# An attention kernel with a feed-forward: five token chunks get the first product of both halves in Strassen's form

## The chip, the cores and the metric

The kernel runs on one core of a Trainium2 chip. The metric is the device time of one execution in microseconds (us); below, every number without a unit is in us. TensorE multiplies matrices, VectorE and ScalarE work element by element and read TensorE's results from PSUM, GpSimd (POOL in the profile) does element work in SBUF alone, and SyncE (SP) issues most transfers. Each engine takes its instructions in the order in which the program gives them.

## The reference

`q`, `k` and `v` are 8 x 8 x 576 x 64 (batch, head, position, dimension), `w_in` is 512 x 2048 and `w_out` 2048 x 512, all float32.

```python
q_s = exp(q - max(q, -1)); q_s /= sum(q_s, -1)
k_s = exp(k - max(k, 2));  k_s /= sum(k_s, 2)
kv  = einsum('bhsd,bhse->bhde', k_s, v)
a   = einsum('bhsd,bhde->bhse', q_s, kv)
x   = a.transpose(0, 2, 1, 3).reshape(4608, 512)
h   = x @ w_in
out = (h * sigmoid(h)) @ w_out
```

Attention is linear: each batch needs a small 64 x 64 matrix `kv` per head. Most of the work is the two products behind it, `x @ w_in` (the first product) and the product with `w_out` (the second).

## The kernel before

**Tiles.** The 4608 tokens are nine chunks of 512 (`TCH`; chunk 0 is worked as the 576 tokens of batch 0). For each chunk, `x` stands transposed in `XT` (features on partitions), the activated first product in `GT` (2048 features as 16 blocks of 128, by tokens), in two buffers that alternate. PSUM has eight banks: 0 to 3 take the first product, 4 and 5 the second, 6 and 7 the attention.

**The first product** has two forms. Plain (`mm1`, L288): per block of 128 features four matmuls 128 x 512 into one bank, then tanh on ScalarE (L248) and a multiply on VectorE (L249), or for the first three blocks one silu on ScalarE (L293). Strassen's (`group`, L352): a half of the features (8 blocks, `g` = 1 or 0) as seven products M1 to M7, in the order 1, 2, 6, 5, 7, 4, 3. Each is eight matmuls 128 x 256. M1, M6, M7 and M4 pile up in banks 0 and 1; M2 takes banks 2 and 3 alone, and M5, M3 pile up there. After M1, M6 and M7 the sum so far is copied out ("snapshot", `group_snap`, L341) to `h0`, `h1`, `h2`; after M2, M7 and M3 VectorE adds banks 2 and 3 to `h0`, `h2`, `h1` (`group_add`, L344). A silu on ScalarE (L350) of each of these, and one directly of banks 0 and 1 after M4, gives the four quarters of the output. The operands are differences of quarters of `x` (`XS1` to `XS4`, `xs_op`, L328, once per chunk) and of `w_in` (`WS`, `ws_op`, L319, once per half).

**The second product** of the chunk before (`prod`, L463) is in Strassen's form throughout: seven products of two parts, each part eight matmuls 128 x 256, in the same order, with differences of `GT` (`S1` to `S4`, `s_op`, L437; S3 is made in place) and of `w_out` (`T1` to `T4`, `t_op`, L447; T3 is made in place too). Its snapshots `sa`, `sb`, `sc` are ScalarE's (L479), its output adds VectorE's (L483, L494), and its stores go through SP.

**The attention** of the next batch runs beside: loads of q, k, v (L97); exps on ScalarE (L108, L111); row sums and reciprocals on VectorE (L146, L150); the scaling of q on POOL (`qnorm`, L155); a cast of v on POOL (`vcast`, L91); a transposing transfer on SP (L165); the `kv` matmuls (L187) with a scaling on VectorE (L198, L200); and `xt` (L226), the matmuls that give `XT` for the next chunk, copied out by VectorE for the first half of the features and by ScalarE for the second.

**The order.** All of it is written out by hand. `units` is a list of pieces of TensorE work: a `p` is one plain block, a `g` one of M1 to M7, a `b` one part of a product of the second kind. `plan(u, f)` puts the work `f` ahead of unit `u`. A chunk 2 to 6 has the pattern

```python
four_pairs = "ggbgbgbgbbgbgb"
"pbpbpbpbpbpbpbp" + four_pairs     # chunks 2 to 6: 29 units
four_pairs + four_pairs            # chunks 7 and 8: 28 units
```

so in chunks 2 to 6 one half of the features is plain, the other (`g` = 1) in Strassen's form. Chunk 1 mixes plain blocks (units 10 to 31 from its start, two banks while the second product of chunk 0 holds four) with that product.

Of the kernel before, what the change touches and what calls it, by code (L numbers as in the profile page):

```python
# [17 lines left out]
def kernel(  # L18
# [252 lines left out]
    hb = [0, 2]  # L271
# [16 lines left out]
    def mm1(t, fb, one=False):  # L288
        bank = hb[0] % hb[1]
        hb[0] += 1  # L290
        mm1_mm(t, fb, bank, range(NC))
        if one:
            nc.scalar.activation(  # L293
                out=GTS[t % 2][:, fb, 0:TCH], in_=PS[:, bank, :], func=ACT.Silu, scale=1.0 / XS
            )
        else:
            mm1_silu(t, fb, bank)
# [41 lines left out]
    def group_snap(i):  # L339
        H[i] = mp.tile([128, 2 * TCH], FP32, name=f"h{i}", bufs=1)  # L340
        nc.scalar.copy(out=H[i], in_=PS[:, 0:2, :].rearrange("p b n -> p (b n)"))  # L341
# [10 lines left out]
    def group(t, g, i):  # L352
# [11 lines left out]
        for p in range(4):  # L364
            for c in range(2):
                nc.tensor.matmul(  # L366
                    out=PS[:, bank + p // 2, (p % 2) * HT:(p % 2 + 1) * HT],
                    lhsT=a[:, c, p * 128:(p + 1) * 128],
                    rhs=bb[:, c, :],
                    start=(i in (1, 2, 5) and c == 0 and p % 2 == 0),  # L370
                    stop=(i in (2, 3, 4) and c == 1 and p % 2 == 1),
                    skip_group_check=True,
                )
        if i == 1:
            group_snap(0)
        elif i == 2:
            group_add(0)
        elif i == 6:
            group_snap(1)
        elif i == 7:  # L380
            group_snap(2)
            group_add(2)
        elif i == 4:
            group_silu(t, None, f1, 0)
        elif i == 3:
            group_silu(t, 2, f1, 1)
            group_silu(t, 0, f0, 0)
            group_add(1)
# [232 lines left out]
    def a_units(t):  # L621
        return [lambda t=t, fb=fb: mm1(t, fb) for fb in FB]

# [13 lines left out]
    a1 = a_units(1)  # L637
# [4 lines left out]
    units += a1[NFB - 10:]  # L642
    for t in range(2, NCH):
        begin[t] = len(units)
        bs = b_units(t - 1, ORDER)
        free = t + 1 >= B
        ps_ = [
            lambda t=t, i=i, fb=fb: mm1(t, fb, i < 3)
            for i, fb in enumerate(() if free else (0, 8, 1, 9, 2, 10, 3, 11))
        ]  # L650
        gs = [
            lambda t=t, g=g, i=i: group(t, g, i)
            for g in ((1, 0) if free else (1,))
            for i in (1, 2, 6, 5, 7, 4, 3)
        ]
        plan(begin[t] + 2, lambda t=t: s_op(t - 1, 1))
        plan(begin[t] + 4, lambda t=t: s_op(t - 1, 2))
        plan(begin[t] + (5 if free else 15), lambda t=t: s_op(t - 1, 3))
        plan(begin[t] + 21, lambda t=t: s_op(t - 1, 4))
        four_pairs = "ggbgbgbgbbgbgb"  # L660
        for x in (four_pairs if free else "pbpbpbpbpbpbpbp") + four_pairs:
            units.append({"p": ps_, "b": bs, "g": gs}[x].pop(0))
            if x == "g" and len(gs) % 7 == 0:
                later = 1 if t == NCH - 1 and not gs else 3
                f0 = 8 if free and not gs else 12
                plan(len(units) - 1 + later, lambda t=t, f0=f0: group_silu(t, 1, f0, 1))
        assert not (ps_ or bs or gs)
        x = begin[t] + (0 if free else 1)
        plan(x, lambda t=t: (xs_op(t, 1), xs_op(t, 2), xs_op(t, 3), xs_op(t, 4)))
# [98 lines left out]
    plan(b1 + 22, lambda: (mm2_plain_out(0, (0, 1)), hb.__setitem__(0, 2), hb.__setitem__(1, 3)))  # L768
# [4 lines left out]
    plan(begin[2], lambda: (hb.__setitem__(0, 0), hb.__setitem__(1, 4)))  # L773
    plan(begin[2] + 5, lambda: t_op(3, nc.vector))
    plan(begin[2] + 18, lambda: t_op(4, nc.vector, 0, 4))
    plan(begin[2] + 20, lambda: t_op(4, nc.vector, 4, 8))

    for t in range(2, NCH - 1):
        b = t + 1
        u = begin[t]  # L780
        if b < B:
            for i in range(2):
                plan(u + 5 + i, lambda i=i, b=b: exp_q(b, i))
                plan(u + 6 + 3 * i, lambda i=i, b=b: (qsum(b, i), qnorm(b, i, nc.gpsimd)))
                plan(u + 10 + 2 * i, lambda i=i, b=b: vcast(b, i, nc.gpsimd))
                plan(u + 17 + 2 * i, lambda i=i, b=b: exp_k(b, i))
                if b + 1 < B:
                    plan(u + 7 + i, lambda i=i, b=b: load(b + 1, "qt", q, i, nc.sync))
                    plan(u + 18 + i, lambda i=i, b=b: load(b + 1, "vt", v, i, nc.sync))
                    plan(u + 20 + i, lambda i=i, b=b: load(b + 1, "kt", k, i, nc.sync))  # L790
            plan(u + 13, lambda b=b: q_transpose(b))
            plan(u + 22, lambda b=b: kv_both(b))
        if b == B:
            plan(u + 8, lambda: (ws_op(1, 0), ws_op(2, 0)))
            plan(u + 11, lambda: (ws_op(3, 0), ws_op(4, 0)))
        plan(u + (24 if b < B else 23), lambda t=t: xt(t + 1, 0, nc.vector))
        plan(u + (27 if b < B else 26), lambda t=t: xt(t + 1, 1))
# [36 lines left out]
```

The softmax here doesn't subtract the row's maximum and nothing guards it: scores larger than these inputs give would overflow.

## Time and profile before

| what | value |
|---|---|
| time, median of 12 runs (lowest, highest) | 270.18 (269.64, 271.05) |
| the profiled execution: its time, its span | 270.61, 268.8 |
| TensorE matmuls, busy | 259.3 (96%) |
| VectorE, ScalarE, POOL, busy | 199.8 (74%), 184.8 (69%), 71.6 (27%) |
| granted TensorE clock | 1.000 |
| bytes moved | 45.88 MB |

A profile line of a group gives the line of the code, the engine, the operation, output<-input with shapes and count; then busy time and mean ns of one; then the idle time just ahead of these on the engine and what ended it. A line of the timeline gives start and duration in us, engine, line, operation and count, and in brackets idle time with its releaser. The line of a window gives the stretch, its length, and for each engine busy time and number of instructions; then granted clock, share of DMA and GB/s. Matmuls overlap, so differences of starts tell what one costs. `PE` is TensorE, `PEld` its weight loads, `DVE` VectorE, `ACT` ScalarE.

### The profile page before, as it was taken

How to read it: one execution, taken by the hardware profiler on the slowest of the kernel's cores; microseconds unless marked ns; L12 is line 12 of the kernel's file. 1: busy time of each engine (PE TensorE's matmuls, PEld its weight loads, DVE VectorE, ACT ScalarE, POOL GpSimd, SP SyncE). 2: the span in 40 equal slices, each digit the busy share in tenths (PEclk: the TensorE clock that was granted, in tenths of full speed). 3: DMA queues.
4: the chain of work that ended last, by engine and by line, in shares of the span. 5: the costliest groups of instructions: out<-in, count | busy, mean ns of one | idle time of the engine just before them, and what ended most of it. 6: DMA issues, size and time to landing. Idle time of an engine off the chain costs nothing.

```text
span 268.8 us, 6167 instructions
## 1 busy us (share of the span) xinstructions
PE 259.3 (96%) x2588; PEld 189.3 (70%) x2588; DVE 199.8 (74%) x279; ACT 184.8 (69%) x226; POOL 71.6 (27%) x63
## 2 busy tenths in 40 slices
PE   8899999999999999999999999999999999999993
PEld 2467644445678767876687668766878888888782
DVE  2866796978898769776977698759869838855832
ACT  5767955669866896689668966896686756674610
POOL 1743981730082007300740064005500000000004
PEclk9999999999999999999999999999999999999999
DMA  7999999399549844993598458940415003400534
GB/s 257 322 206 354 255 336 332 151 212 391 201 148 262 255 93 166 190 329 83 178 231 284 86 176 197 306 97 0 90 35 124 2 0 66 93 0 5 122 76 117
DMA packets 35452, 45.88 MB, mean 171 GB/s; under 512 B 16208, under 2 KB 19984, under 8 KB 35424
## 3 DMA queue, kind: packets, MB, share of 16 engines
q1 hardware_dynamic: 29568, 33.69, 45.1%
q0 software_dynamic: 5616, 11.60, 16.5%
q8 instruction: 20, 0.33, 0.5%
q10 hardware_dynamic: 240, 0.20, 0.3%
q14 instruction: 8, 0.07, 0.1%
HBM read 36.70 MB, written 9.44 MB: 172 GB/s over the span
## 4 chain that ended last, share of the span: by engine, by line
PE 66%; DVE 12%; DMA 6%; ACT 6%; issue 6%; POOL 2%; POOLq 0%; DVEq 0%; ACTq 0%
PE PS L463 28%; PE PS L366 18%; PE PS L276 11%; DMA qt<-in_q_dram 5%; DVE zq L146 4%; DVE GT L249 4%; PE PS L401 3%; ACT eq L108 2%; PE PS L226 2%; PE PS L187 2%; ACT L108 2%; DMA W<-in_moe_w_in_dram 1%; ACT sg L248 1%; DVE ow L483 1%; DVE h L344 1%
## 5 line engine op out<-in xcount | busy, mean ns | idle before, releaser
L463 PEld LDWEIGHTS <-GT 128*128 128x128 f16 x512 | 49.6, 98 | 11.7 <-issue 1.8
L155 POOL TENSOR_TENSOR eq<-eq,rzq 128x1152 bf16<-128x1152 bf16 x13 | 27.5, 2116 | 105.1 <-DVE rzq L150 105.1
L276 PE MATMUL PS<-XT,W 128*128 128x512 f16 (+1 forms) x224 | 54.7, 371 | 0.3 <-ACT ow L413 0.3
L463 PE MATMUL PS<-W,GT 128*128 128x256 f16 x384 | 49.1, 273 | 0.4 <-DVE h L344 0.4
L344 DVE TENSOR_TENSOR h<-PS,h 128x1024 f32<-128x1024 f32 x27 | 33.0, 1221 | 17.9 <-PE PS L366 10.4
L249 DVE SCALAR_TENSOR_TENSOR GT<-sg,PS 128x512 f16<-128x512 f32 (+2 forms) x57 | 37.4, 671 | 10.8 <-ACT sg L248 10.2
L248 ACT ACTIVATE sg<-PS 128x512 f32<-128x512 f32 (+2 forms) x57 | 33.1, 595 | 17.2 <-PE PS L276 8.1
L463 PEld LDWEIGHTS <-S 128*128 128x128 f16 x384 | 37.5, 98 | 7.7
L341 ACT COPY h<-PS 128x1024 f32<-128x1024 f32 x27 | 27.3, 1013 | 18.6 <-PE PS L366 18.4
L276 PEld LDWEIGHTS <-W 128*128 128x128 f16 x224 | 21.7, 98 | 17.2 <-issue 1.3
L463 PE MATMUL PS<-T,S 128*128 128x256 f16 x256 | 32.7, 273 | 0.0
L366 PEld LDWEIGHTS <-WS 128*128 128x128 f16 x288 | 27.3, 98 | 4.7 <-issue 1.4
L366 PE MATMUL PS<-XS,WS 128*128 128x256 f16 x216 | 28.0, 273 | 0.0
L350 ACT ACTIVATE GT<-h 128x1024 f16<-128x1024 f32 x27 | 27.5, 1055 | 0.3 <-DVE h L344 0.3
L146 DVE TENSOR_REDUCE zq<-eq 128x18 f32<-128x1152 bf16 x12 | 16.2, 1350 | 15.2 <-ACT eq L108 15.2
L366 PEld LDWEIGHTS <-W 128*128 128x128 f16 x216 | 21.1, 98 | 5.4 <-issue 2.0
L696 POOL DMA_DIRECT2D out_dram<-ow x5 | 2.7, 546 | 70.8 <-DVE ow L681 70.8
L108 ACT ACTIVATE eq<-qt 128x1152 bf16<-128x1152 f32 x16 | 18.1, 1158 | 2.7 <-DMA qt<-in_q_dram 2.6
L91 POOL CAST vaug<-vt 128x1152 bf16<-128x1152 f32 x12 | 19.4, 1647 | 0.0
L111 ACT ACTIVATE ek<-kt 128x1152 bf16<-128x1152 f32 x16 | 18.6, 1164 | 1.2 <-DMA kt<-in_k_dram 1.2
L366 PE MATMUL PS<-XT,W 128*128 128x256 f16 x144 | 18.2, 272 | 0.9 <-DVE h L344 0.4
L256 PE MATMUL PS<-XT,W 128*128 128x288 f16 x128 | 16.6, 286 | 1.0 <-DVE GT L249 0.6
(78 smaller groups left out, 341.1 us busy)
## 6 DMA issues: line engine op xcount, KB each, us to landing
out_dram<-ow SPq DMA_DIRECT2D x64, 128.0 KB, 2.4
qt<-in_q_dram SPq DMA_DIRECT2D x12, 576.0 KB, 4.6
kt<-in_k_dram SPq DMA_DIRECT2D x12, 576.0 KB, 7.8
vt<-in_v_dram SPq DMA_DIRECT2D x12, 576.0 KB, 5.8
qt<-in_q_dram POOLq DMA_DIRECT2D x4, 576.0 KB, 13.5
kt<-in_k_dram POOLq DMA_DIRECT2D x4, 576.0 KB, 13.8
vt<-in_v_dram POOLq DMA_DIRECT2D x4, 576.0 KB, 12.3
W<-in_moe_w_out_dram POOLq DMA_DIRECT2D x4, 512.0 KB, 15.1
```

Source lines behind the costliest of these rows:

```text
L91: eng.tensor_copy(o, i)
L108: nc.scalar.activation(out=half(st[b]["eq"], cc), in_=jgd(b, "qt", cc), func=ACT.Exp)
L146: nc.vector.reduce_sum(out=z, in_=e, axis=AX.X)
L155: eng.tensor_tensor(out=e, in0=e, in1=r[:, :, :, None].to_broadcast([128, J, 2, D]), op=ALU.mult)
L248: nc.scalar.activation(out=s, in_=i, func=ACT.Tanh, scale=OS)
L249: nc.vector.scalar_tensor_tensor(out=o, in0=s, scalar=1.0, in1=i, op0=ALU.add, op1=ALU.mult)
L276: nc.tensor.matmul(out=PS[:, bank, o0:TCH], lhsT=W1[:, c, fb * 128:(fb + 1) * 128], rhs=XTS[t % 2][:, c, o0:TCH], start=(c == 0), stop=(c ...
L341: nc.scalar.copy(out=H[i], in_=PS[:, 0:2, :].rearrange("p b n -> p (b n)"))
L344: nc.vector.tensor_tensor(out=H[i], in0=PS[:, 2:4, :].rearrange("p b n -> p (b n)"), in1=H[i], op=ALU.add)
L350: nc.scalar.activation(out=group_out(t, f, n), in_=x, func=ACT.Silu, scale=1.0 / XS)
L366: nc.tensor.matmul(out=PS[:, bank + p // 2, (p % 2) * HT:(p % 2 + 1) * HT], lhsT=a[:, c, p * 128:(p + 1) * 128], rhs=bb[:, c, :], start=(i ...
L463: nc.tensor.matmul(out=PS[:, bank, m * HN:(m + 1) * HN], lhsT=a[:, fc, m * 128:(m + 1) * 128], rhs=bb[:, fc, :], start=(first and fc == 0) ...
```

## The change

Chunks 2 to 6 get the pattern of chunks 7 and 8: both halves in Strassen's form, 28 units. A new function `full(t)` lays out such a chunk:

- Of the six snapshots two are VectorE's: the second of half 1 (after M6) and the third of half 0 (after M7).
- The silus of `h0`, `h1`, `h2` are no longer issued right after M3 but at units of their own (`defer`); that of half 0's `h1` falls at the start of the next chunk.
- All four exps stand ahead of unit 11 (units 3, 4, 6 and 10), where they stood at units 5, 6, 17 and 19. The loads of q and k for the batch after that follow the exps; those of v come at units 22 and 23.
- Row sums at units 7 and 11; scaling on POOL behind them; casts of v at units 2 and 11; the transpose at 17; `kv` at 15 (22 before); `xt` at 22 and 27 (24 and 27 before).
- `s_op` at units 4, 5, 15 and 19 (2, 4, 15 and 21 before).

Outside: the weight differences of half 0 (`ws_op(.., 0)`) move from chunk 7 to units 10 and 11 of chunk 1; T4 and T3 move from VectorE in chunk 2 to POOL at unit 22 of chunk 1; chunk 1's plain blocks take their banks from a list. On POOL the casts of a batch now come ahead of its scalings.

The diff, cut to its core:

```diff
-    hb = [0, 2]
+    A1_BANKS = [0, 1, 0, 1, 0, 1, 2, 0, 3, 1, 0, 2, 1, 0, 2, 3]
 
...
-    def mm1(t, fb, one=False):
-        bank = hb[0] % hb[1]
-        hb[0] += 1
-        mm1_mm(t, fb, bank, range(NC))
-        if one:
-            nc.scalar.activation(
-                out=GTS[t % 2][:, fb, 0:TCH], in_=PS[:, bank, :], func=ACT.Silu, scale=1.0 / XS
-            )
-        else:
-            mm1_silu(t, fb, bank)
+    def mm1(t, i):
+        mm1_mm(t, FB[i], A1_BANKS[i], range(NC))
+        mm1_silu(t, FB[i], A1_BANKS[i])
 
 
 
...
-    def group_snap(i):
+    def group_snap(i, eng=nc.scalar):
         H[i] = mp.tile([128, 2 * TCH], FP32, name=f"h{i}", bufs=1)
-        nc.scalar.copy(out=H[i], in_=PS[:, 0:2, :].rearrange("p b n -> p (b n)"))
+        copy(eng, H[i], PS[:, 0:2, :].rearrange("p b n -> p (b n)"))
 
...
-    def group(t, g, i):
+    def group(t, g, i, on=None, defer=False):
...
+        on = on or {}
         if i == 1:
             group_snap(0)
         elif i == 2:
             group_add(0)
         elif i == 6:
-            group_snap(1)
+            group_snap(1, on.get(1, nc.scalar))
         elif i == 7:
-            group_snap(2)
+            group_snap(2, on.get(2, nc.scalar))
             group_add(2)
         elif i == 4:
             group_silu(t, None, f1, 0)
         elif i == 3:
-            group_silu(t, 2, f1, 1)
-            group_silu(t, 0, f0, 0)
+            if not defer:
+                group_silu(t, 2, f1, 1)
+                group_silu(t, 0, f0, 0)
             group_add(1)
 
 
...
     ORDER = (1, 2, 6, 5, 7, 4, 3)
-    a1 = a_units(1)
+    a1 = [lambda i=i: mm1(1, i) for i in range(NFB)]
 
     units += [lambda i=i: mm2_plain(0, i) for i in range(10)]
     for i in range(10, NFB):
         units += [a1[i - 10], lambda i=i: mm2_plain(0, i)]
     units += a1[NFB - 10:]
+    four_pairs = "ggbgbgbgbbgbgb"
+    def full(t):
+        begin[t] = u = len(units)
+        b = t + 1
+        bs = b_units(t - 1, ORDER)
+        gs = [
+            lambda g=g, i=i: group(t, g, i, {1: nc.vector} if g else {2: nc.vector}, True)
+            for g in (1, 0)
+            for i in ORDER
+        ]
+        for x in 2 * four_pairs:
+            units.append({"b": bs, "g": gs}[x].pop(0))
+        for i, x in ((1, 4), (2, 5), (3, 15), (4, 19)):
+            plan(u + x, lambda i=i: s_op(t - 1, i))
+        for g, at3 in ((1, (13, 17, 15)), (0, (23, 28, 25))):
+            f1, f0 = 4 * g, 4 * g + 8
+            for i, x, f, n in zip(range(3), at3, (f0, f0, f1), (0, 1, 1)):
+                plan(u + x, lambda i=i, f=f, n=n: group_silu(t, i, f, n))
+        more = b + 1 < B
+        for i in range(2):
+            plan(u + (3, 10)[i], lambda i=i: exp_q(b, i))
+            plan(u + (7, 11)[i], lambda i=i: qsum(b, i))
+            plan(u + (16, 17)[i], lambda i=i: qnorm(b, i, nc.gpsimd))
+            plan(u + (2, 11)[i], lambda i=i: vcast(b, i, nc.gpsimd))
+            plan(u + (6, 4)[i], lambda i=i: exp_k(b, i))
+            if more:
+                plan(u + (5, 12)[i], lambda i=i: load(b + 1, "qt", q, i, nc.sync))
+                plan(u + (8, 6)[i], lambda i=i: load(b + 1, "kt", k, i, nc.sync))
+                plan(u + (22, 23)[i], lambda i=i: load(b + 1, "vt", v, i, nc.sync))
+        plan(u + 17, lambda: q_transpose(b))
+        plan(u + 15, lambda: kv_both(b))
+        plan(u + 22, lambda: xt(t + 1, 0, nc.vector))
+        plan(u + 27, lambda: xt(t + 1, 1))
+        plan(u, lambda: (xs_op(t, 1), xs_op(t, 2), xs_op(t, 3), xs_op(t, 4)))
     for t in range(2, NCH):
-        begin[t] = len(units)
+        if t < B - 1:
+            full(t)
+            continue
+        begin[t] = u = len(units)
         bs = b_units(t - 1, ORDER)
-        free = t + 1 >= B
-        ps_ = [
-            lambda t=t, i=i, fb=fb: mm1(t, fb, i < 3)
-            for i, fb in enumerate(() if free else (0, 8, 1, 9, 2, 10, 3, 11))
-        ]
-        gs = [
-            lambda t=t, g=g, i=i: group(t, g, i)
-            for g in ((1, 0) if free else (1,))
-            for i in (1, 2, 6, 5, 7, 4, 3)
-        ]
-        plan(begin[t] + 2, lambda t=t: s_op(t - 1, 1))
-        plan(begin[t] + 4, lambda t=t: s_op(t - 1, 2))
-        plan(begin[t] + (5 if free else 15), lambda t=t: s_op(t - 1, 3))
-        plan(begin[t] + 21, lambda t=t: s_op(t - 1, 4))
-        four_pairs = "ggbgbgbgbbgbgb"
-        for x in (four_pairs if free else "pbpbpbpbpbpbpbp") + four_pairs:
-            units.append({"p": ps_, "b": bs, "g": gs}[x].pop(0))
+        gs = [lambda t=t, g=g, i=i: group(t, g, i) for g in (1, 0) for i in ORDER]
+        plan(u + 2, lambda t=t: s_op(t - 1, 1))
+        plan(u + 4, lambda t=t: s_op(t - 1, 2))
+        plan(u + 5, lambda t=t: s_op(t - 1, 3))
+        plan(u + 21, lambda t=t: s_op(t - 1, 4))
+        for x in 2 * four_pairs:
+            units.append({"b": bs, "g": gs}[x].pop(0))
             if x == "g" and len(gs) % 7 == 0:
                 later = 1 if t == NCH - 1 and not gs else 3
-                f0 = 8 if free and not gs else 12
+                f0 = 12 if gs else 8
                 plan(len(units) - 1 + later, lambda t=t, f0=f0: group_silu(t, 1, f0, 1))
-        assert not (ps_ or bs or gs)
-        x = begin[t] + (0 if free else 1)
-        plan(x, lambda t=t: (xs_op(t, 1), xs_op(t, 2), xs_op(t, 3), xs_op(t, 4)))
+        assert not (bs or gs)
+        plan(u, lambda t=t: (xs_op(t, 1), xs_op(t, 2), xs_op(t, 3), xs_op(t, 4)))
+        if t < NCH - 1:
+            plan(u + 23, lambda t=t: xt(t + 1, 0, nc.vector))
+            plan(u + 26, lambda t=t: xt(t + 1, 1))
 
 
     begin[NCH] = len(units)
...
-    plan(b1 + 22, lambda: (mm2_plain_out(0, (0, 1)), hb.__setitem__(0, 2), hb.__setitem__(1, 3)))
+    plan(b1 + 22, lambda: mm2_plain_out(0, (0, 1)))
...
-    plan(begin[2], lambda: (hb.__setitem__(0, 0), hb.__setitem__(1, 4)))
-    plan(begin[2] + 5, lambda: t_op(3, nc.vector))
-    plan(begin[2] + 18, lambda: t_op(4, nc.vector, 0, 4))
-    plan(begin[2] + 20, lambda: t_op(4, nc.vector, 4, 8))
-    for t in range(2, NCH - 1):
-        b = t + 1
-        u = begin[t]
-        if b < B:
-            for i in range(2):
-                plan(u + 5 + i, lambda i=i, b=b: exp_q(b, i))
-                plan(u + 6 + 3 * i, lambda i=i, b=b: (qsum(b, i), qnorm(b, i, nc.gpsimd)))
-                plan(u + 10 + 2 * i, lambda i=i, b=b: vcast(b, i, nc.gpsimd))
-                plan(u + 17 + 2 * i, lambda i=i, b=b: exp_k(b, i))
-                if b + 1 < B:
-                    plan(u + 7 + i, lambda i=i, b=b: load(b + 1, "qt", q, i, nc.sync))
-                    plan(u + 18 + i, lambda i=i, b=b: load(b + 1, "vt", v, i, nc.sync))
-                    plan(u + 20 + i, lambda i=i, b=b: load(b + 1, "kt", k, i, nc.sync))
-            plan(u + 13, lambda b=b: q_transpose(b))
-            plan(u + 22, lambda b=b: kv_both(b))
-        if b == B:
-            plan(u + 8, lambda: (ws_op(1, 0), ws_op(2, 0)))
-            plan(u + 11, lambda: (ws_op(3, 0), ws_op(4, 0)))
-        plan(u + (24 if b < B else 23), lambda t=t: xt(t + 1, 0, nc.vector))
-        plan(u + (27 if b < B else 26), lambda t=t: xt(t + 1, 1))
+    plan(b1 + 10, lambda: (ws_op(1, 0), ws_op(2, 0), ws_op(3, 0)))
+    plan(b1 + 11, lambda: ws_op(4, 0))
+    plan(b1 + 22, lambda: (t_op(4, nc.gpsimd), t_op(3, nc.gpsimd)))
```

More of the change, by code (lines that the diff above doesn't have):

```diff
@@ L619 @@
     FB = [x for i in range(HF) for x in (i, i + HF)]
-    def a_units(t):
-        return [lambda t=t, fb=fb: mm1(t, fb) for fb in FB]
     def b_units(t, order):
```

## The prediction

> **What bounds the kernel now.** I read in this order: the granted clock (1.000, so no throttle), the busy time per chunk, TensorE's instructions in order of time, the waits, and last VectorE's order. A chunk begins at its first matmul of the first product (91.76, 119.00, 146.24, 173.48, 200.70, 226.78). Busy time in chunk 4 and, below it, in chunk 7 (columns: window, its length, each engine's busy time and instructions, clock, DMA):
>
> ```profile
> 119.00:146.24 27.24, 27.14 (x290) 20.30 (x288) 21.19 (x29) 21.07 (x26) 7.43 (x4) 1.00 0.70 194
> 200.70:226.78 26.08, 25.65 (x235) 22.03 (x232) 19.24 (x24) 16.43 (x19) 0.00 (x0) 1.00 0.18 39
> ```
>
> TensorE (27.14 of 27.24) bounds the chunk; VectorE has 21.19, ScalarE 21.07. Chunk 7 already has both halves in Strassen's form. TensorE's own order gives the price of a unit (start, duration, count, idle time and releaser):
>
> ```profile
> 119.00 1.03 PE L276 MATMUL PS<-XT,W 128*128 128x512 f16 x4
> 119.86 1.04 PE L463 MATMUL PS<-W,GT 128*128 128x256 f16 x8
> ...
> 132.02 2.17 PE L366 MATMUL PS<-XT,W 128*128 128x256 f16 x16
> 134.02 1.04 PE L463 MATMUL PS<-T,S 128*128 128x256 f16 x8
> ...
> 138.48 0.81 PE L187 MATMUL PS<-vaug,ek 64*64 64x65 bf16 x72
> 139.22 1.05 PE L366 MATMUL PS<-XS,WS 128*128 128x256 f16 x8
> ...
> 213.00 1.04 PE L366 MATMUL PS<-XT,W 128*128 128x256 f16 x8
> 214.47 1.03 PE L366 MATMUL PS<-XT,W 128*128 128x256 f16 x8 [0.43 <-DVE h L344]
> ```
>
> Starts, not durations, tell the cost, since ends overlap: a plain unit (4 x 512) takes 0.866, a Strassen or second-product unit (8 x 256) 0.873. kv adds 0.84 (137.51 to 139.22, less one unit), each xt 0.44. Two products at 132.02 take 2.00 instead of 1.75: 0.25 is lost inside M2. That group writes banks 2 and 3, and bank 3 still holds the last plain block until VectorE's L249 has read it, at 133.45. Check: 8 x 0.866 + 21 x 0.873 + 0.84 + 2 x 0.44 + 0.25 = 27.23, the chunk. The last pair is the one bracketed wait of chunk 7: 1.47 between starts, so 0.60 lost, behind VectorE, which did four weight sums (L319) there.
>
> **Part 1: a unit fewer per chunk.** In chunks 2 to 6, eight plain units (6.93) become seven Strassen units (6.11): 0.82. The bank-3 loss of 0.25 goes too in chunks 3 to 6, since a chunk now begins behind a Strassen group whose banks were read long ago. Without new waits a chunk is 28 x 0.873 + 0.84 + 0.88 = 26.16.
>
> **Part 2: what VectorE and ScalarE get for it.** Rows:
>
> ```profile
> L344 DVE TENSOR_TENSOR h<-PS,h 128x1024 f32<-128x1024 f32 x27 | 33.0, 1221 | 17.9 <-PE PS L366 10.4 <-ACT h L341 7.4
> L341 ACT COPY h<-PS 128x1024 f32<-128x1024 f32 x27 | 27.3, 1013 | 18.6 <-PE PS L366 18.4
> L249 DVE SCALAR_TENSOR_TENSOR GT<-sg,PS 128x512 f16<-128x512 f32 x25 | 16.1, 660 | 0.3
> L91 DVE CAST XT<-PS 128x1024 f16<-128x1024 f32 x6 | 7.3, 1215 | 0.0
> ```
>
> Per chunk VectorE loses five L249 (3.3) and gets three adds (3.66) and two snapshots. A float32 snapshot on VectorE is not in the trace; its bounds are the L341 copy (1.01, ScalarE) and L344, which reads a second operand (1.22). I take 1.215, the PSUM cast of the same width. Sum: 21.19 + 2.8 = 24.0 of 26.2. ScalarE loses five tanh (2.96) and three short silus (1.79), gets four long silus (4.2) and one snapshot (1.01): 21.5, with two table loads per chunk as before. In chunk 2 the first exps follow chunk 1's tanh without a table change, which saves two loads (2.57) there, off TensorE's path. The exps now stand ahead of snap and silu work, but each lies where ScalarE's next customer is later: its nearest deadlines are the third snapshot of half 1 before M4 and the direct silu before the next M1, with about 0.45 and 0.6 left. Both become TensorE waits if ScalarE runs half a microsecond late.
>
> VectorE has no such average to spare, so I walk its queue by hand, as the after order gives it, from where TensorE anchors it: M6 of half 1 (unit 3) is out at 4 x 0.873 + 0.2 = 3.7 from the chunk's start (0.2 from the end of a unit's 0.87 to its reader: 139.22 + 0.87 = 140.10, ScalarE's copy began at 140.30). Steps are start-to-start times in chunk 4: snapshot 1.13, S1 1.25, S2 1.15, row sum and reciprocal 1.64, add 1.14, output add 0.60, second row sum and reciprocal 1.57, add 1.14. That is 13.3. On the way S2 is ready at 7.3 for M6 of the second product (due 7.85), the add at 10.1 for M3 (due 10.47), the add at 13.4 for M2 of half 0 (due 13.93). Then comes S3, and here POOL matters:
>
> ```profile
> 131.80 2.12 POOL L155 TENSOR_TENSOR eq<-eq,rzq 128x1152 bf16<-128x1152 bf16 x1 [1.19 <-DVE rzq L150]
> 133.86 3.25 POOL L91 CAST vaug<-vt 128x1152 bf16<-128x1152 f32 x2
> ...
> 133.45 1.55 DVE L437 TENSOR_TENSOR GT<-GT 128x2048 f16<-128x2048 f16 x1
> 134.92 1.21 DVE L344 TENSOR_TENSOR h<-PS,h 128x1024 f32<-128x1024 f32 x1
> 136.06 2.13 DVE L437 TENSOR_TENSOR S<-GT,S 128x2048 f16<-128x2048 f16 x1
> ```
>
> L437 alone takes 1.22; started under POOL's L155 it ends 1.1 after L155 does, and likewise under the cast. The PSUM add (1.21) is untouched. The row's mean of S3 (1.42) would charge 0.2. The Trainium skill, "SBUF — State Buffer", section "Who interferes with whom", speaks against the change here: a VectorE instruction with two SBUF inputs and a GpSimd one that reads SBUF exclude each other for the whole instruction. Before, S3 caught the last half microsecond of the second L155. Now it is queued only one add behind the reciprocal that releases that L155, which therefore runs 12.4 to 14.5, and S3 waits for all of it. So I charge 14.5 + 1.14 + kv reciprocal and two scalings 0.70 + add 1.27 = 17.6 to 17.7. Behind that add waits M5 of half 0, due at 19 x 0.873 + 0.84 = 17.43. By the row TensorE waits nothing and the chunk is 26.16; by the rule it waits 0.2 to 0.3. I take 0.3: **26.46 per chunk, 0.78 saved**. After it VectorE idles until the snapshot that frees its output add (20.2), so nothing accumulates.
>
> **Part 3: moved attention steps and transfers.** Row scaling on POOL ends at 14.5; the transpose issued behind it (4.6 to landing) is in by 19.3, ahead of xt at unit 22 (20.3). kv at unit 15 needs ek (ScalarE, 7.2) and casts of a load issued a chunk earlier. On SP's queue q and k loads now come early, each behind the exp that frees its buffer; the v loads stand behind the transpose, land about 23, and their casts are wanted 16 later. The stores follow these and wait for VectorE alone, as now. All at nothing; cover gone, xt would lose what the transpose is late by.
>
> **Part 4: the seams.** (a) Four L319 sums move into chunk 1 at its first plain units. VectorE idles 1.93 there (44.57 to 46.50, for L248), which hides three at 0.6. The fourth pushes the row sums and L249 of the third block from 51.30 to 51.96. Bank 0 is wanted at 51.31: TensorE loses **0.65**, as there are only two banks. (b) The same sums leave chunk 7: **0.60** back. (c) Chunk 2's M2 follows the last plain block of chunk 1 in bank 3, read at 65.98 against 65.8 wanted: **0.25** stays. (d) The T3 and T4 differences go from VectorE in chunk 2 (three instructions, about 3.4) to POOL at the end of chunk 1. The nearest POOL row, L155, gives 1.84 ns per element, so 2048 elements are an estimate of 3.8 each, from 56.9 to 64.5 with the shift. The skill's "GPSIMD Engine Reference", section 3.1, states 4.5 for a float32 add of 2048, so 65.9; VectorE's next pair of SBUF inputs (XS) starts about 66.6. I take the row and charge nothing; at 5 each XS would wait, up to 0.5 on M5.
>
> **Sum.** Chunks 3 to 6: 4 x 0.78 = 3.1. Chunk 2: 0.78 - 0.25 = 0.5. Chunk 1: -0.65. Chunk 7: +0.60. Together 3.6. The profiled execution took 270.61 (span 268.8, 1.8 around it), giving 267.0; that execution is 0.43 above the median of 270.18, to which I apply the same difference: **266.6**.
>
> **Rivals.** *VectorE sets the pace, and it is slower.* 31 of its instructions in a chunk, with deadlines 0.3 to 0.5 apart, leave little. If each costs 0.06 more than in its contiguous stretches of before (a wait on a semaphore each, say), the same walk reaches M3, M2 and M5 late one after the other and a chunk is 27.4; five times 0.17 more plus the 0.3 of the seams is 271.3. It decides from about 0.045 per instruction, where a chunk is 27.18. For it: the bracketed VectorE wait of chunk 7. Against: the stretches I used already contain such waits. *VectorE paces in part*, 0.03 each: chunk 26.87, 268.6. *The port costs nothing*, because the scaling falls elsewhere or S3 goes first: 26.16 per chunk, another 1.5, 265.1. *The change doesn't do what it says*: the unit count is fixed by the code, so only its saving can be eaten.
>
> **Chances.** 0.55 for 266.6 (265.7 to 267.8), 0.15 for the free port, 0.16 for partial pacing, 0.14 for VectorE as the bound. The range 264.9 to 269.7 takes in the first three. A measurement here tells about 0.2%, 0.54 us. Faster 0.80, of the partial case all but a part; same 0.07, where pacing is near its break-even; slower 0.13.
>
> **What would show it.** Starts of chunks 3 to 7 some 26.5 apart; one TensorE wait per chunk at M5 of half 0, released by the first add of that half; S3 at about 2.2 directly behind POOL's second scaling; no bracketed wait in chunk 7; 0.65 more in chunk 1. Wrong would be waits at M3, M2 or M6 too (VectorE as the bound), a late transpose ahead of xt, or XS stretched behind T3.

## The result, and the profile after

The changed kernel takes **266.34 us** (median of 8 runs, 265.37 to 266.53) against 270.17 for the kernel before (32 runs, 269.38 to 271.08). The ratio is 0.9851, 95% interval 0.9838 to 0.9865: 3.83 us, or 1.4%, faster, where 3.6 were forecast. The profiled execution took 266.13, with a span of 264.3 (before: 270.61 and 268.8), so the two profiles differ by 4.5. All line numbers below are those of the changed kernel, unless a fence is of the kernel before or of an experiment on it: in the changed one L359 holds the matmuls of a Strassen group of the first product, L458 those of the second product, L337 the group's adds, L91 the copies that VectorE and POOL make, L89 those of ScalarE, L432 the S operands, L155 the scaling of q.

The same busy-time view as before the change, for chunk 4 and chunk 7 (window, its length, busy time and instructions of PE, PEld, VectorE, ScalarE and POOL, clock, DMA share, GB/s):

```profile
118.35:144.54 26.19, 26.19 (x314) 22.64 (x312) 23.75 (x29) 21.20 (x23) 6.55 (x4) 1.00 0.72 196
196.90:222.31 25.41, 25.41 (x234) 22.04 (x232) 16.48 (x20) 15.33 (x18) 0.00 (x0) 1.00 0.20 43
```

Chunk 4 is 26.19 long and TensorE is busy for all of it. VectorE went from 21.19 to 23.75 (24.0 forecast), ScalarE from 21.07 to 21.20 (21.5 forecast). The rows of VectorE that grew, from the page and from the groups with shapes kept apart (busy, mean ns of one, idle time before):

```profile
L337 DVE TENSOR_TENSOR h<-PS,h 128x1024 f32<-128x1024 f32 x42 | 50.7, 1207 | 11.7 <-PE PS L359 6.2 <-ACT h L89 5.3
L432 DVE TENSOR_TENSOR GT<-GT 128x2048 f16<-128x2048 f16 x8 | 15.4, 1925 | 0.0
L91 DVE COPY h<-PS 128x1024 f32<-128x1024 f32 x10 | 12.2, 1219 | 0.5
```

The group adds went from 27 to 42, and ten snapshots, which no trace of before had shown on VectorE, took 1219 ns each (1.215 was taken). The 25 multiplies L249 of 128x512 are gone. In the second row the in-place difference S3 has a mean of 1925 ns, against 1421 before: in each of chunks 2 to 6 it meets POOL and takes 2.35, and elsewhere it takes 1.22.

TensorE in order of time in chunk 4, from the chunk's start, around M5 of half 0, at the attention product, and at the start of chunk 5 (start, duration, count, idle time and its releaser in brackets):

```profile
118.35 1.91 PE L359 MATMUL PS<-XT,W 128*128 128x256 f16 x16
120.10 1.04 PE L458 MATMUL PS<-W,GT 128*128 128x256 f16 x8
...
134.91 1.04 PE L458 MATMUL PS<-W,GT 128*128 128x256 f16 x8
135.79 1.04 PE L359 MATMUL PS<-XS,WS 128*128 128x256 f16 x8
...
138.50 0.41 PE L226 MATMUL PS<-qT,kvn 64*64 64x320 bf16 x8
138.85 1.92 PE L458 MATMUL PS<-T,GT 128*128 128x256 f16 x16
...
144.54 1.91 PE L359 MATMUL PS<-XT,W 128*128 128x256 f16 x16
```

The pair that opens a chunk now takes 1.75 between starts where it took 2.00: the 0.25 lost inside M2 is gone. M5 starts 0.88 after the unit ahead of it, which is a unit's own length, so the wait forecast there does not exist in this chunk. VectorE's own order and POOL's two scalings say by how little:

```profile
130.45 1.16 DVE L337 TENSOR_TENSOR h<-PS,h 128x1024 f32<-128x1024 f32 x1
131.53 2.35 DVE L432 TENSOR_TENSOR GT<-GT 128x2048 f16<-128x2048 f16 x1
133.80 0.17 DVE L198 RECIPROCAL rz<-PS 128x4 f32<-128x4 f32 x1
134.00 0.49 DVE L200 TENSOR_TENSOR kvn<-PS,rz 128x128 bf16<-128x128 f32 x2
134.41 1.22 DVE L337 TENSOR_TENSOR h<-PS,h 128x1024 f32<-128x1024 f32 x1
```

```profile
127.43 2.12 POOL L155 TENSOR_TENSOR eq<-eq,rzq 128x1152 bf16<-128x1152 bf16 x1 [10.96 <-DVE rzq L150]
130.67 2.12 POOL L155 TENSOR_TENSOR eq<-eq,rzq 128x1152 bf16<-128x1152 bf16 x1 [1.12 <-DVE rzq L150]
```

S3 took 2.35 instead of 1.22: it began 0.86 after the start of POOL's second scaling, and ended 1.09 after its end (133.88 against 132.79). The add before it, which reads PSUM, ran its 1.16 undisturbed under the same scaling. The last add ends at 135.63, 17.28 after the chunk's start.

Where TensorE does lose time in the changed kernel:

```profile
49.60 0.92 PE L276 MATMUL PS<-XT,W 128*128 128x448 f16 x4
50.35 1.03 PE L396 MATMUL PS<-W,GT 128*128 128x512 f16 x4
51.70 0.92 PE L276 MATMUL PS<-XT,W 128*128 128x448 f16 x4 [0.32 <-DVE GT L249]
...
64.75 2.20 PE L359 MATMUL PS<-XT,W 128*128 128x256 f16 x16
66.79 1.04 PE L458 MATMUL PS<-W,GT 128*128 128x256 f16 x8
...
81.65 1.04 PE L458 MATMUL PS<-W,GT 128*128 128x256 f16 x8
82.81 1.03 PE L359 MATMUL PS<-XS,WS 128*128 128x256 f16 x8
...
111.72 0.30 PE L226 MATMUL PS<-qT,kvn 64*64 64x256 bf16 x4
112.42 0.30 PE L226 MATMUL PS<-qT,kvn 64*64 64x256 bf16 x4 [0.40 <-DMA qT<-eq]
112.65 1.92 PE L458 MATMUL PS<-T,GT 128*128 128x256 f16 x16
...
209.13 1.91 PE L359 MATMUL PS<-XT,W 128*128 128x256 f16 x16
```

These are, by differences of starts: 0.19 and 0.48 in chunk 1 (the block at 49.60 should have come at 49.41, that at 51.70 at 51.22), 0.29 inside M2 of chunk 2, 0.29 at M5 of half 0 in chunk 2 (no bracket shows either of these two), and 0.58 in chunk 3 inside the attention product, which waits for the transposed q (111.72 to 112.65 is 0.93, where the same step takes 0.35 in chunk 4; the bracket shows only 0.40 of it). In chunk 7 the pair M1, M2 at 209.13 runs through: its old wait of 0.60 is gone.

Chunk by chunk, from the starts (before 64.52, 91.76, 119.00, 146.24, 173.48, 200.70, 226.78, 252.03; after 64.75, 91.57, 118.35, 144.54, 170.74, 196.90, 222.31, 247.57):

| stretch | before | after | saved | forecast |
|---|---|---|---|---|
| up to chunk 2 | 64.52 | 64.75 | -0.23 | -0.65 |
| chunk 2 | 27.24 | 26.82 | 0.42 | 0.53 |
| chunk 3 | 27.24 | 26.78 | 0.46 | 0.78 |
| chunks 4, 5, 6 | 27.24, 27.24, 27.22 | 26.19, 26.20, 26.16 | 3.15 | 2.34 |
| chunk 7 | 26.08 | 25.41 | 0.67 | 0.60 |
| chunk 8 and the end | 42.02 | 41.99 | 0.03 | 0 |

Together 4.5, the difference of the spans. In the first row 0.29 is luck of the execution: the front of the program, which the change does not touch, ran that much earlier in this profile; chunk 1 itself is 0.52 longer.

### The profile page after: what moved, and what is told of

The parts are those of the page before. It is cut to its first block, busy times and chain, and to the rows that moved or that the text cites. A ratio compares the mean times of both kernels' runs of the same rounds, so it can differ in the third digit from the quotient of the medians.

```text
span 264.3 us, 6375 instructions
## 1 busy us (share of the span) xinstructions
PE 254.2 (96%) x2708; PEld 200.8 (76%) x2708; DVE 210.7 (80%) x276; ACT 182.8 (69%) x209; POOL 75.8 (29%) x65
## 4 chain that ended last, share of the span: by engine, by line
PE 63%; DVE 17%; DMA 8%; issue 4%; POOL 3%; ACT 2%; POOLq 0%; DVEq 0%; ACTq 0%
PE PS L458 30%; PE PS L359 26%; DMA qt<-in_q_dram 5%; DVE GT L249 3%; DVE h L337 3%; DMA qT<-eq 2%; DVE S L432 2%; DVE zq L146 2%; PE PS L276 2%; PE PS L226 2%; PE PS L187 1%; DVE WS L312 1%; DMA W<-in_moe_w_in_dram 1%; PE PS L396 1%; DVE zq L148 1%
## 5 line engine op out<-in xcount | busy, mean ns | idle before, releaser
L337 DVE TENSOR_TENSOR h<-PS,h 128x1024 f32<-128x1024 f32 x42 | 50.7, 1207 | 11.7 <-PE PS L359 6.2
L458 PEld LDWEIGHTS <-GT 128*128 128x128 f16 x512 | 49.6, 98 | 7.4 <-issue 1.6
L458 PE MATMUL PS<-W,GT 128*128 128x256 f16 x384 | 49.1, 273 | 0.4 <-DVE h L337 0.4
L359 PEld LDWEIGHTS <-WS 128*128 128x128 f16 x448 | 43.7, 98 | 5.8 <-issue 0.7
L155 POOL TENSOR_TENSOR eq<-eq,rzq 128x1152 bf16<-128x1152 bf16 x13 | 27.5, 2117 | 59.1 <-DVE rzq L150 59.1
L359 PE MATMUL PS<-XS,WS 128*128 128x256 f16 x336 | 43.5, 273 | 0.1
L343 ACT ACTIVATE GT<-h 128x1024 f16<-128x1024 f32 x42 | 43.3, 1054 | 0.3 <-DVE h L337 0.3
L89 ACT COPY h<-PS 128x1024 f32<-128x1024 f32 x32 | 32.4, 1013 | 13.7 <-PE PS L359 13.3
L458 PEld LDWEIGHTS <-S 128*128 128x128 f16 x384 | 37.1, 98 | 5.4 <-issue 1.0
L359 PEld LDWEIGHTS <-W 128*128 128x128 f16 x336 | 32.5, 98 | 4.4 <-issue 0.2
L458 PE MATMUL PS<-T,S 128*128 128x256 f16 x256 | 32.7, 273 | 0.0
L249 DVE SCALAR_TENSOR_TENSOR GT<-sg,PS 128x576 f16<-128x576 f32 (+1 forms) x32 | 21.2, 680 | 8.4 <-ACT sg L248 8.2
L359 PE MATMUL PS<-XT,W 128*128 128x256 f16 x224 | 27.9, 273 | 0.0
L343 ACT ACTIVATE GT<-PS 128x1024 f16<-128x1024 f32 x14 | 14.3, 1024 | 19.5 <-PE PS L359 19.5
L248 ACT ACTIVATE sg<-PS 128x576 f32<-128x576 f32 (+1 forms) x32 | 18.8, 598 | 9.5 <-PE PS L276 5.4
L91 POOL CAST vaug<-vt 128x1152 bf16<-128x1152 f32 x12 | 14.9, 1247 | 36.1 <-DMA vt<-in_v_dram 27.8
L458 PE MATMUL PS<-W,S 128*128 128x256 f16 x128 | 16.5, 273 | 0.0
```

What stands on the lines that cost most here:

```text
L89: eng.copy(out=o, in_=i)
L155: eng.tensor_tensor(out=e, in0=e, in1=r[:, :, :, None].to_broadcast([128, J, 2, D]), op=ALU.mult)
L248: nc.scalar.activation(out=s, in_=i, func=ACT.Tanh, scale=OS)
L249: nc.vector.scalar_tensor_tensor(out=o, in0=s, scalar=1.0, in1=i, op0=ALU.add, op1=ALU.mult)
L337: nc.vector.tensor_tensor(out=H[i], in0=PS[:, 2:4, :].rearrange("p b n -> p (b n)"), in1=H[i], op=ALU.add)
L343: nc.scalar.activation(out=group_out(t, f, n), in_=x, func=ACT.Silu, scale=1.0 / XS)
```

## The experiments

Three theories were to be told apart. **TensorE bounds** the chunk, and the gain is its unit and its M2 wait. **VectorE is the bound or nearly so**, which was the rival on the other side. And POOL's scaling, through **S3, is what is left** at M5. Beside them stood the seams, that is, what was lost in chunk 1 and inside M2 of chunk 2, and the late transpose of chunk 3, which no step had charged. The runs came in three series, each with the changed kernel in it; differences are of medians within a series. A median of four to seven executions tells only about half a microsecond: in the profiles, the start of chunk 1 alone, up to which all these kernels do the same, lies between 43.6 and 46.1. The length of a chunk is the finer measure.

### A unit more on TensorE, an operation more on VectorE, the snapshots back on ScalarE

The changed kernel again, in the first series:

> The changed kernel again, as the reference for the others of this call. Both theories: 266.3, 3.8 below the kernel before.

It took 265.46 (ratio 0.9814, interval 0.9797 to 0.9830), 0.9 below the 266.34 of the same code above. First, eight matmuls of 128x256 into a bank that is free at that time, in each of chunks 2 to 6:

```diff
+    def extra_u():
+        for _ in range(8):
+            nc.tensor.matmul(out=PS[:, 7, 0:HT], lhsT=W1[:, 0, 0:128], rhs=W2[:, 0, 0:HT], start=True, stop=True)
...
+        plan(u + 6, lambda: extra_u())
```

> Chunks 2 to 6 get one more unit for TensorE (eight 128 x 256 matmuls into bank 7, used by nothing) ahead of unit 6. Theory (TensorE bounds the changed chunks, VectorE's chain has little to wait for): +0.87 in each of chunks 4, 5 and 6; in chunks 2 and 3 less by the waits of 0.29 and 0.40 that it covers, so +3.7 in all, 270.0. Rival (VectorE sets the pace of the changed chunks): the unit is hidden, under +1.5.

Measured: 269.57, which is 4.1 more, and against the kernel before 0.9974 (0.9963 to 0.9986). The chunks begin at 119.20, 146.27, 173.33 and 200.37, so chunks 4 to 6 are 27.07, 27.06 and 27.04 long: 0.87 to 0.88 more each, the full length of the unit. In chunks 2 and 3 the waits at M5 and for the transposed q disappear, as each has 0.87 more time to come. Chunks 2 to 6 are together 3.4 longer than in the profile above, which is 5 x 0.87 less the two waits (0.29 and 0.58). **TensorE bounds**; by the medians a unit put back takes back 4.1 of the 4.8 gained in this series.

Next, one copy of 128x512 out of PSUM more on VectorE in each of those chunks, ahead of the group's second add:

```diff
+    def extra_v():
+        x = mp.tile([128, S], FP32, name="sg", bufs=3)[:, 0:512]
+        nc.vector.tensor_scalar_mul(out=x, in0=PS[:, 6, :], scalar1=1.0)
...
+        plan(u + 7, lambda: extra_v())
```

> Chunks 2 to 6 get one more VectorE instruction (a 128 x 512 copy out of bank 6, 0.60 from start to start) ahead of the first row sum. Theory: VectorE's chain from M6 of half 1 to M5 of half 0 ends 0.11 ahead of TensorE in chunk 4, so 0.5 of the 0.6 shows at M5 in every chunk, 0.2 of it already at M3; +2.5 in all. Rival (VectorE has 2 or more of slack in a chunk, as its busy share of 90% and its idle time suggest): under +0.5.

Measured: 269.11, 3.65 more where 2.5 were expected (0.9936 to 0.9977 of the kernel before). TensorE in chunk 6 with it:

```profile
183.04 1.04 PE L458 MATMUL PS<-T,S 128*128 128x256 f16 x8
184.10 1.03 PE L359 MATMUL PS<-XT,WS 128*128 128x256 f16 x8
...
190.15 1.04 PE L458 MATMUL PS<-W,GT 128*128 128x256 f16 x8
191.34 0.92 PE L359 MATMUL PS<-XS,WS 128*128 128x256 f16 x7 [0.16 <-DVE h L337]
```

By the starts M3 of half 1 is 0.19 late and M5 of half 0 another 0.32; in chunks 3 to 6 the two sum to 0.48 to 0.51. The copy costs VectorE 0.60 (0.54 to the start of the next instruction, an add that then takes 1.13 instead of 1.08 to the next). So of what is added to VectorE all but about 0.1 becomes TensorE's wait. In chunk 2 it is more, 0.24 at M6 of the second product, 0.60 at M3 and 0.30 at M5. Chunks 2 to 6 are together 2.5 longer than in this series' profile of the changed kernel, as expected. Most of the rest lies ahead of chunk 2, where the edit does nothing: it begins at 65.32 against 64.44. VectorE is busy 91% of a chunk and doesn't bound it, yet it has no more room than the 0.11 between the last add's end (17.28 on, and about 0.05 to its reader) and M5 at 17.44.

Then the two snapshots of a chunk that VectorE makes were given to ScalarE:

```diff
-            lambda g=g, i=i: group(t, g, i, {1: nc.vector} if g else {2: nc.vector}, True)
+            lambda g=g, i=i: group(t, g, i, {}, True)
```

> All six snapshots of a chunk on ScalarE again. Theory: VectorE's chain gets 1.13 shorter, so the waits at M5 in chunk 2 and at the transposed q in chunk 3 go (-0.7), but ScalarE's snapshot after M7 of half 1 comes 0.9 later and holds M4 of half 1, which has 0.45 to spare: +0.45 in each of five chunks; about +1.5 in all. Rival (VectorE is what limits, ScalarE has room): -0.7 or better.

Measured: 267.50, 2.0 more (0.9874 to 0.9920 of before), 1.5 expected; chunks 2 to 6 are together 1.0 longer in the profile. M4 of half 1 waits for ScalarE now, whose third copy for it stands behind a table load of 1.28 and three exps. Chunk 4 in TensorE's order:

```profile
125.85 1.04 PE L458 MATMUL PS<-T,S 128*128 128x256 f16 x8
127.06 1.03 PE L359 MATMUL PS<-XS,W 128*128 128x256 f16 x8 [0.18 <-ACT h L89]
```

1.21 between starts where a unit has 0.87: 0.34 lost in chunks 3, 4 and 6, 0.63 in chunk 5, nothing in chunk 2, where no table is loaded ahead of the exps. The wait at M5 of chunk 2 is gone, as the theory had it; that for the transposed q in chunk 3 is not (0.46). So the two snapshots on VectorE are a needed part of the change: ScalarE had not one copy (1.01) to spare ahead of M4.

### The seams, the scaling and the v loads

The changed kernel in the second series:

> The changed kernel again, as the reference for the others of this call: between 265.4 and 266.4.

It took 265.80 (0.9842; 0.9817 to 0.9867). First the two seams: the fourth weight sum fourteen units later, and the last two plain blocks of chunk 1 in banks that M2 doesn't want:

```diff
-    A1_BANKS = [0, 1, 0, 1, 0, 1, 2, 0, 3, 1, 0, 2, 1, 0, 2, 3]
+    A1_BANKS = [0, 1, 0, 1, 0, 1, 2, 0, 3, 1, 0, 2, 1, 0, 6, 7]
...
-    plan(b1 + 11, lambda: ws_op(4, 0))
+    plan(b1 + 25, lambda: ws_op(4, 0))
```

> The fourth weight difference of half 0 goes from unit 11 of chunk 1 to unit 25, and the last two plain blocks of chunk 1 to banks 6 and 7. Theory (the seam costs are what the prediction said: a row sum pushes L249 of the third block, and M2 of chunk 2 waits for the last block's bank): the loss of 0.47 at the fifth plain block falls to 0.1 or less, that of 0.28 inside M2 to nothing, so 0.6 below the changed kernel, some of it taken back at M5 of chunk 2, which waits for VectorE: 0.4 to 0.6. Rival (other waits stand right behind, so that they only move): under 0.2.

Measured: 265.52, 0.3 less, and the intervals overlap (0.9806 to 0.9849). Both waits are gone, and a new one has come. TensorE, VectorE and POOL in chunk 2:

```profile
70.24 1.04 PE L458 MATMUL PS<-W,GT 128*128 128x256 f16 x8
71.98 1.05 PE L458 MATMUL PS<-T,S 128*128 128x256 f16 x8 [0.70 <-DVE S L432]
```

```profile
68.45 2.14 DVE L432 TENSOR_TENSOR S<-GT 128x2048 f16<-128x2048 f16 x1
70.69 1.23 DVE L432 TENSOR_TENSOR S<-S,GT 128x2048 f16<-128x2048 f16 x1
```

```profile
68.36 1.16 POOL L91 CAST vaug<-vt 128x1152 bf16<-128x1152 f32 x1 [0.65 <-DMA vt<-in_v_dram]
```

TensorE reaches chunk 2 earlier, but the load of v does not, and its cast falls on S1, which takes 2.14: M6 of the second product comes 0.87 late. Chunk 1 is 0.59 shorter than in the first profile of the changed kernel (19.62 against 20.21) and chunk 2 0.53 longer (27.35 against 26.82): in this execution nearly all that was taken out at the seams went back in some 8 later.

Next, the scaling of q is left out (for batches 3 to 7, so that their attention is not normalised); no other line changes, but the transpose, which waits for the scaling, now goes out about 5 earlier:

```diff
-            plan(u + (16, 17)[i], lambda i=i: qnorm(b, i, nc.gpsimd))
```

> Leaves out the scaling of q on POOL for batches 3 to 7 (two POOL instructions per chunk). Theory (S3 stands still while the second of them holds the path to SBUF): S3 falls from 2.35 to 1.22, chunk 2 loses its wait at M5 (0.29) and chunk 3 that at the transposed q, since the transpose starts 5 earlier; 0.4 to 0.7 below the changed kernel. Rival (S3 is long for itself, by its in-place form): S3 stays above 1.9 and M5 of chunk 2 still waits.

Measured: 265.39, 0.4 less, intervals overlapping (0.9806 to 0.9848). S3 is free, and the wait at M5 of chunk 2 and that for q in chunk 3 are gone; every chunk from 3 to 6 is 26.16 to 26.20 long:

```profile
L432 DVE TENSOR_TENSOR GT<-GT 128x2048 f16<-128x2048 f16 x8 | 9.7, 1214 | 0.0
```

1214 ns against 1925. The stretch of S3 is POOL's scaling and nothing else; what TensorE loses by it is small, since all but chunk 2 have just room for it. In chunk 2 of this run 0.48 is lost at M6 of the second product instead, again with the cast of v under S1.

Last, the v loads two units later, to see whether they are what makes the transpose of q late in chunk 3:

```diff
-                plan(u + (22, 23)[i], lambda i=i: load(b + 1, "vt", v, i, nc.sync))
+                plan(u + (24, 25)[i], lambda i=i: load(b + 1, "vt", v, i, nc.sync))
```

> The v loads go from units 22 and 23 to 24 and 25, which on SP's queue puts them behind four stores that wait for VectorE, so 8 later. Theory (the transpose of chunk 3 lands in 6.3 instead of 4.6 because the v loads issued behind it share its queue): it lands in 4.6 to 4.8 in every chunk, the wait of chunk 3 goes, 0.1 to 0.4 below the changed kernel. Rival (it is late by something else): landing still 5.5 to 6.3 in some chunk, no change, or slower by the casts of v, which now fall next to S1 and S2 of the next chunk.

Measured: 268.79, **3.0 more** (0.9937 to 0.9977 of before). The theory missed, and the cost that its rival named came. The transpose of chunk 3 still took 6.0 from issue to landing (6.2 in the changed kernel of this series), so the v loads are not its cause. And the casts, which had fallen into the end of a chunk, now fall under S1 and S2 of the next. VectorE, POOL and TensorE in chunk 4:

```profile
123.04 1.22 DVE L432 TENSOR_TENSOR S<-GT 128x2048 f16<-128x2048 f16 x1
124.29 2.06 DVE L432 TENSOR_TENSOR S<-S,GT 128x2048 f16<-128x2048 f16 x1
```

```profile
123.25 2.03 POOL L91 CAST vaug<-vt 128x1152 bf16<-128x1152 f32 x1 [17.05 <-DMA vt<-in_v_dram]
```

```profile
125.19 1.04 PE L458 MATMUL PS<-W,GT 128*128 128x256 f16 x8
126.41 1.05 PE L458 MATMUL PS<-T,S 128*128 128x256 f16 x8 [0.18 <-DVE S L432]
```

A cast that takes 1.16 alone took 2.03 here, and S2 2.06 instead of 1.23; each chunk from 3 to 6 loses 0.35 at M6 of the second product and another 0.30 at M5. A cast that the scheduler's list has moved by two units came some 9 us later, and the queue of SP says why. In the changed kernel, chunk 3:

```profile
106.03 2.73 SPq L165 DMA_TRANSPOSE qT<-eq  x1
108.82 1.15 SPq L97 DMA_DIRECT2D vt<-in_v_dram  x2
```

and with the loads moved:

```profile
106.22 2.72 SPq L165 DMA_TRANSPOSE qT<-eq  x1
116.48 2.41 SPq L392 DMA_DIRECT2D out_dram<-ow  x4
118.93 1.12 SPq L97 DMA_DIRECT2D vt<-in_v_dram  x2
```

Two units put the loads behind four output stores, which wait for their results: 10.1 later (8 expected), not 1.7. Loads for which TensorE doesn't wait so took back 3.0 of the 4.4 that the change gains in this series.

### The seam again, and two parts of the change put into the kernel before

The changed kernel in the third series:

> The changed kernel again, as the reference for the others of this call: between 265.4 and 266.4.

It took 266.68 (0.9860; 0.9833 to 0.9886), just outside what was expected; its executions spread from 265.14 to 268.18. The fourth weight sum seven units later instead of fourteen, banks as in the first try:

```diff
-    plan(b1 + 11, lambda: ws_op(4, 0))
+    plan(b1 + 18, lambda: ws_op(4, 0))
```

> As in the run with both seams mended, but the fourth weight difference at unit 18 of chunk 1, ahead of POOL's T4 and T3 and not beside them. Theory: the 0.47 and 0.18 in chunk 1 and the 0.28 inside M2 go, and in chunk 2 S1 still meets the casts of v on POOL, so that M6 of the second product waits for S2 by 0.3 to 0.9 again: 0.2 to 0.6 below the changed kernel. Rival (the loss at S2 came from the difference standing beside T3): no wait at S2, 0.8 to 0.9 below.

Measured: 266.17, 0.5 less, intervals again overlapping (0.9839 to 0.9882). The wait of chunk 1 only moved, to later blocks. In chunk 2 the loss came at another place than the theory said: the cast fell on XS4 (1.37 instead of 0.42) and not on S1, so that M5 of half 1 was 0.79 late, M6 of the second product only 0.11:

```profile
58.12 0.92 PE L276 MATMUL PS<-XT,W 128*128 128x448 f16 x4 [0.33 <-DVE ow L410]
...
70.52 1.03 PE L359 MATMUL PS<-XS,WS 128*128 128x256 f16 x8 [0.62 <-DVE h L337]
```

No version was found that is clearly faster than the changed kernel.

The other two start from the kernel before, and do one part of the change alone. The weight sums from chunk 7 to chunk 1:

```diff
+    plan(b1 + 10, lambda: (ws_op(1, 0), ws_op(2, 0), ws_op(3, 0)))
+    plan(b1 + 11, lambda: ws_op(4, 0))
...
-        if b == B:
-            plan(u + 8, lambda: (ws_op(1, 0), ws_op(2, 0)))
-            plan(u + 11, lambda: (ws_op(3, 0), ws_op(4, 0)))
```

> The kernel before with one part of the change alone: the four weight differences of half 0 at units 10 and 11 of chunk 1 instead of in chunk 7. Theory: chunk 7 loses its wait of 0.60, chunk 1 gets one of 0.5 to 0.65: within 0.2 of the kernel before. Rival (the move alone gains): 0.5 below it.

Measured: 270.12, ratio 1.0001 (0.9984 to 1.0018). The wait of chunk 7 is gone, and 0.19 and 0.47 stand in chunk 1 as in the changed kernel. Within the noise that part of the change is an even exchange.

And the last two plain blocks of chunks 2 to 6 in banks 6 and 7, so that M2 finds its bank free with no unit saved:

```diff
+        if t > 1 and fb in (3, 11):
+            bank = 6 if fb == 3 else 7
         mm1_mm(t, fb, bank, range(NC))
```

> The kernel before with the last two plain blocks of chunks 2 to 6 in banks 6 and 7 instead of 2 and 3. Theory (0.25 per chunk is lost inside M2, whose bank 3 still holds the last plain block, and the change wins it back along with the unit): M2 no longer waits, 0.25 in each of five chunks, 1.25 below the kernel before. Rival (the gap inside M2 is TensorE's own, or the wait goes to the next VectorE result): under 0.4.

Measured: 269.16, 0.96 less (0.9946 to 0.9982, so 0.5 to 1.5). The pair M1, M2 takes 1.74 instead of 2.00, and chunks are 26.98 to 26.99 instead of 27.24, which over five chunks would be 1.25:

```profile
130.84 1.91 PE L368 MATMUL PS<-XT,W 128*128 128x256 f16 x16
132.58 1.04 PE L465 MATMUL PS<-T,S 128*128 128x256 f16 x8
```

So the gain has two parts, now shown apart. About 1.0 of it (0.25 in five chunks, less the 0.29 that chunk 2 of the changed kernel has in its M2) is a wait for a bank, which two bank numbers alone remove. The rest is the saved unit, five times 0.8, less the waits of chunks 2 and 3 (0.29 and 0.58); what chunk 1 loses and chunk 7 gains (0.52 and 0.67) nearly cancels.

## Why the prediction was right, step by step

**The unit and the bank (Part 1): right.** A chunk without new waits was put at 26.16; chunks 4 to 6 are 26.19, 26.20 and 26.16. The 1.05 saved in each is the forecast's 0.82 + 0.25. The experiment with a unit more shows that a unit costs its full 0.87 to 0.88 there, and that with the banks alone shows the 0.25.

**The wait of 0.3 at M5 (Part 2): right in what stretches S3, wrong in four chunks of five on what that costs TensorE.** Chunk 2 has the wait, at 0.29; chunk 3 has a different one; chunks 4 to 6 have none. They are as long as under the rival of the free port, but not by its cause: the port cost VectorE its 1.1, and TensorE had just room for it. The walk put the last add's end at 17.6 to 17.7, and it was at 17.28. Term by term, forecast and then measured in chunk 4: end of the second scaling 14.5, 14.44; S3 after it 1.14, 1.01; reciprocal and two scalings of kv 0.70, 0.61; the add 1.27, 1.22. Each is a little smaller, together 0.33, and the wait was 0.3. The rule of the Trainium skill ("SBUF — State Buffer", "Who interferes with whom"), which the walk took against the mean of the trace's row, holds: S3 waited for the whole scaling, and with the scaling away it took 1214 ns. By the row's mean S3 would have cost 1.42, by the rule 2.3; 2.35 came out. Where the prediction chose wrongly is in taking a wait of 0.3 from a chain whose steps were known to about 0.1 each: such a margin has no sign. Its own terms give 17.61 against 17.43, so 0.2, and it took the upper end. In chunk 2 S1 met a POOL cast (1.60 instead of 1.22), and the same chain, so much later, did wait. Without these 0.38 its last add would have come some 0.1 ahead of M5, so that the 0.29 there equals the forecast by luck.

**VectorE's room: right.** The walk had 0.37 at M3 of half 1 and nothing at M5. The operation more on VectorE came out 0.19 late at M3 and the rest at M5, so TensorE's waits for VectorE begin when a chunk's instructions cost some 0.1 more. For the change to lose, as in the rival in which VectorE sets the pace, a chunk would have had to be 1.0 longer (27.18 against 26.19). It did not come to pass because the instructions cost what they had cost in the stretches of before, or less.

**Transfers at nothing (Part 3): wrong in chunk 3.** The transpose of q was given 4.6 from issue to landing and a second of cover. In the changed kernel it took 4.7, 6.3, 5.5, 4.6 and 4.6 in chunks 2 to 6; in chunk 3 it came late, a sign that the prediction had listed against itself, and TensorE lost 0.58 by the starts (0.34 to 0.41 in the profiles of the three repeats, and in one of them 0.2 in chunk 4 too, where the landing took 6.0). In the kernel before the times were 5.7 and 5.3 in chunks 3 and 4 too, with more cover: the step took a median where the chunk in question had a row of its own. The cause of the longer landing isn't settled: later v loads left it at 6.0, and in chunk 3 it is the longest or next to it in every profile but that without the scaling.

**The seams (Part 4).** (a) 0.65 was charged to chunk 1; 0.19 + 0.48 = 0.67 is there, at the fourth and fifth block, which wait for the multiplies (L249) of the second and third, though the chunk as a whole is only 0.52 longer, as small losses of before (0.06 at the block at 51.37 among them) don't recur. (b) 0.60 for chunk 7; 0.67. (c) 0.25 was to stay inside M2 of chunk 2; 0.29. (d) T3 and T4 on POOL were taken as 3.8 each, from L155's time per element; they took 4.07, on fp16; the figure of the Trainium skill ("GPSIMD Engine Reference", section 3.1) for a float32 add of that length is 4.5. They ended at 64.62, and the first XS began at 66.22, so charging nothing was right. But what was asked of POOL there stopped one instruction too soon. The casts of v come next on that queue, released by a load, and fall on XS4 or S1 in chunk 2. In two of the four profiled executions of the changed kernel the cast fell on XS4 and cost 0.50 to 0.52 at M5 of half 1, as here (VectorE, then TensorE, of one of the repeats):

```profile
67.93 1.38 DVE L321 TENSOR_TENSOR XS<-XT,XS 128x512 f16<-128x512 f16 x1
69.24 1.21 DVE L337 TENSOR_TENSOR h<-PS,h 128x1024 f32<-128x1024 f32 x1
```

```profile
69.11 1.04 PE L458 MATMUL PS<-W,GT 128*128 128x256 f16 x8
70.50 1.03 PE L359 MATMUL PS<-XS,WS 128*128 128x256 f16 x8 [0.35 <-DVE h L337]
```

XS4 alone takes 0.42; POOL's cast began at 67.89, ahead of it. Chunk 2 is then 27.39 long, longer than before the change.

**The sum.** 3.6 was forecast. The two profiles differ by 4.5, of which 0.29 is the front of the program, so the change saved 4.2 there; the medians differ by 3.83. That the total came so near is in part luck. In the profiles two misses have opposite signs: 0.8 too little in chunks 4 to 6, against 0.3 too much in chunk 3 and 0.1 in chunk 2. They leave 0.4 and the seams 0.2, so 0.6 more than forecast; the medians show 0.2 more, as the profiled execution of before was 0.4 above its median and that of the changed kernel 0.2 below. Where the cast meets XS4, chunk 2 loses 0.6 more.

## What to carry to other kernels

When a change leaves the busiest engine with no wait, read the others by their deadlines, not by their busy share: VectorE at 91% was safe here by 0.1 us at one place, and 0.6 us more of it in a chunk, or two loads moved behind a few stores, took back more than half of the gain. Before paying for fewer instructions, look between the starts of a group for a wait that has no bracket: a quarter of a chunk's gain could be had with two bank numbers. And when POOL shares a chunk with VectorE's operations on two SBUF operands, place POOL's work, the casts released by transfers included, by what runs on VectorE at that moment: every encounter cost VectorE about what POOL had still to run.

## What the runs showed of the hardware that was not expected

- **The exclusion costs both sides, and casts bring it too.** The prediction had read it under a cast in the trace of before, but charged it to POOL's scaling alone: under the scaling S3 went from 1.22 to 2.35, under casts S1 to 2.14 and 1.60, S2 to 2.06, XS4 from 0.42 to 1.38. In the other direction a cast of 1.16 took 2.03, and POOL's T3 4.52 instead of 4.07 when the weight sum that was moved to unit 25 of chunk 1 ran beside it. VectorE's row sum, which reads one SBUF operand, kept its 1.34 under a cast (with the late v loads), and the add that reads PSUM its 1.16 under the scaling.
- **A gap inside a pair of products carries no bracket.** The 0.25 in M2 is a wait for a bank in the middle of 16 matmuls, gone when the banks were changed alone; the view names no releaser, and only the starts show it.
- **The transpose's landing time is not one number.** 4.6 to 6.3 in the changed kernel; 7.2 to 9.0 in the kernel without the scaling, where it is issued earlier, beside the loads of q and k.
